# Eighteen scatters of token places put behind the late rows' match matrices, and one expert's input transposes one block later

## The chip, the cores and the metric

The kernel runs on one core of one Trainium2 chip. The metric is device microseconds (us) of one execution, as the median of three runs. TensorE is called PE here, its weight loads PEld, VectorE DVE, ScalarE ACT, GpSimd POOL, and SyncE SP; SP issues most DMAs, POOL issues the indirect ones (a list of rows in, a list of rows out).

## What is computed

Three layers in a row: masked attention (4 batches, 8 heads, 576 positions, head size 64), a mixture of eight experts of which each token takes one, and a two-layer network with a squared ReLU. Cut to what matters:

```python
x = attn_out.transpose(0, 2, 1, 3).reshape(B * S, H * D)     # 2304 tokens x 512
logits = x @ w_gate
e_idx = np.argmax(logits, axis=1)                             # one expert per token
gate_w = softmax(logits)[np.arange(N), e_idx]
eom = 1.0 / (1.0 + np.exp(-(x @ w_output_gate)))
for e in range(E):
    mask = e_idx == e
    h = np.maximum(x[mask] @ w1[e], 0.0)
    out[mask] = gate_w[mask, None] * eom[mask, e, None] * (h @ w2[e])
h = np.maximum(out @ w_in, 0.0)
return h * h @ w_out
```

## The kernel before

**Attention and routing.** Attention runs batch after batch. Its output stays on chip as `xT`; whenever the heads of 128 tokens are done, `gates()` (L555) turns them into rows (`rw`, L568), copies them to `xr`, stores them to the DRAM table `x_d` (L595, SP queue) and reduces the routing logits (`lg`, L572). There are 18 such tiles of 128 tokens in four groups, 0 to 3, 4 to 8, 9 to 12 and 13 to 17. `route()` (L786) takes a group: it finds each token's expert, its place in that expert's bucket (`rk`, `pp`, `posi`, L810 to L825), and queues one **scatter** per tile in the list `scq`: a POOL indirect DMA (L860) that writes 128 token numbers, 4 bytes each, to their places in the DRAM table `tab_d`.

**When a scatter is issued.** `put_place()` (L530) takes one from the list. A scatter of group 0 or 1 stands behind a one-column POOL copy `seen` (L451) that reads a tile of batch 2 or 3, so the first four come in batch 2's attention and the next five in batch 3's. The nine of groups 2 and 3 stand behind `lead["win"]`, the last gather of the first expert's rows.

**The first expert.** Experts run in an order found at run time, largest first, in slots 0 to 7. For slot 0 nothing is read back from `tab_d`: once group 2 is routed, `match_rows()` (L638) computes the first 416 places on PE, and four POOL gathers (`win`, L613) fetch rows from `x_d` into the four `win` buffers. The tokens of group 3 come late: `late_rows()` (L729) compares their places with the places of the slot and makes one **match matrix** `pm` per tile (DVE, L735); PE adds the matched rows up in `lr` (L753, L766), and the split `xh`, `xl` of those sums lets slot 0's first matmul start.

**The next experts.** A slot is eight F1 blocks `f`. In each, `e_l1` makes 12 matmuls to `h` (L1105 to L1107 through a helper), and `e_l2` of two blocks before makes 12 to `y`. At (slot 0, f=1) SP reads slot 1's token list from `tab_d` (`rows_of`, L609), which waits for every scatter; then POOL gathers slot 1's rows (L613), in three tiles of up to 128, and behind them clears `y2T` (L1292, POOL), which the end of slot 0 writes first (L1228). At f=5 of slot 0 `win_split(1)` (L1176) turns the gathered rows over on PE (`wt`, L1183) and splits them into `xh`, `xl` (ACT L1185, DVE L1186) for slot 1's first block. For the later slots this is at f=4.

**What sets the order.** The framework orders each engine's queue by data dependences, program order and its own estimate of times; `tc.issue_after(x)` keeps an instruction behind `x` on its engine. A queue, once ordered, runs strictly in that order: whoever waits holds all behind it. SP's queue carries the weight loads (`rw`, L1079), the early loads of the last layer's weights (`e6wi`, L1120) and the token lists.

Of the kernel before, what the change touches and what calls it, by code (L numbers as in the profile page):

```python
# [20 lines left out]
P = 128  # L21
# [111 lines left out]
def moe_kernel(ctx, tc, q, k, v, wg, wog, w1, w2, w_in64, w_out64, consts, out, dbg=None):  # L133
# [174 lines left out]
    cnt_ev = [0]  # L308
    last_ev, ev_ = {}, [None]
    behind = {}  # L310

    def evac(out_ap, in_ap, scale=None):
        cnt_ev[0] += 1
        if EVP[cnt_ev[0] % len(EVP)]:
            if scale is None:
                ev_[0] = ("v", nc.vector.tensor_copy(out_ap, in_ap))
            else:
                nc.vector.tensor_scalar(out_ap, in_ap, scale, None, op0=ALU.mult)
        else:
            ev_[0] = ("s", nc.scalar.activation(out_ap, in_ap, AF.Copy, scale=1.0 if scale is None else scale))  # L320

# [106 lines left out]
    def unit_s(b, t, u):  # L428
# [19 lines left out]
        )  # L448
        if u == 1 and b >= 2:
            seen = wk.tile([P, 1], F32, name=f"seen{b}", tag="seen", bufs=1)  # L450
            behind[b - 2] = nc.gpsimd.tensor_copy(seen, flat(pr)[:, 0, 0:1])  # L451
        return None, pn
# [60 lines left out]
    q2, q3 = [], []  # L513
    done_all = [False]

    def drain(n2, n3):
        while len(q2) > n2:
            q3.append(unit2(*q2.pop(0)))
        while len(q3) > n3:
            a = q3.pop(0)  # L520
            unit3(*a)
            last_ev[ev_[0][0]] = ev_[0][1]
            done.add((a[0], a[2], a[3]))
            gates()
            if done_all[0]:
                while scq:
                    put_place()


    def put_place():  # L530
        fn, g = scq.pop(0)
        with tc.issue_after((behind[g] if g < 2 else lead["win"]).ins):
            fn()

# [194 lines left out]
    def late_rows(t0, t1, rows):  # L729
# [3 lines left out]
        for t in range(t0, t1):  # L733
# [3 lines left out]
            )  # L737
            pms.append((t, pm))
        with tc.issue_after(lead["pm"].ins):
            while lows:  # L740
# [45 lines left out]
    def route(b, ts, lg, rows):  # L786
# [84 lines left out]
        for i, t in enumerate(ts):  # L871
            scq.append((lambda i=i, t=t: scatter(i, t), b))

# [11 lines left out]
    for b in range(B):  # L885
        t = tiles[b]
        tn = transposes(b + 1, tiles[b + 1]) if b + 1 < B else iter(())
        for n, ku in enumerate(ORDER[b].split()):
# [22 lines left out]
            if b == B - 1 and n >= LN and early and "do" in lead:  # L911
                lead.pop("do")()
                early_load()
                lead["ok"] = 1
            for _ in range(2):
                if scq and (scq[0][1] in behind if scq[0][1] < 2 else "ok" in lead):
                    put_place()
            for _ in range(TN[b][n]):
# [4 lines left out]
        if b + 2 < B:  # L923
            tiles[b + 2] = load(b + 2)
    done_all[0] = True
    while scq:
        put_place()
    drain(0, 0)


# [347 lines left out]
    for k in range(E):  # L1278
        for f in range(NF1):
# [18 lines left out]
            if (k, f) in CONV:  # L1298
# [4 lines left out]
                for j in range(n * len(halves) // len(CONV), (n + 1) * len(halves) // len(CONV)):  # L1303
                    conv_early(j)
            if f == (5 if k == 0 else 4) and k + 1 < E:
                win_split(k + 1)
# [290 lines left out]
```

## Time and profile before

| what | before |
|---|---|
| median of three runs | 801.55 us (800.99 to 802.63) |
| the profiled execution's own time | 803.88 us |
| its span, first to last instruction | 802.1 us |
| PE busy, share of the span | 95% |
| DVE, ACT, POOL busy | 68%, 57%, 24% |
| attention and routing | until about 168 us |
| eight expert slots, then the last layer | from about 168 us |

The profile is one execution. The page gives the busy time of each engine and the chain of work that ended last; the views of the trace give the instructions in order of time, what ended the idle time before each, and busy time by stretch. Times in them are us from the span's start.

### The profile page before, as it was taken

Reading aid. Unit: us, or ns where it says so; the run is one execution under the profiler, and the core shown is the slowest. Engines: PE = TensorE matmul, PEld = TensorE weight load, DVE = VectorE, ACT = ScalarE, POOL = GpSimd, SP = SyncE. Lnnn points to the kernel's source line nnn. Section 1 sums busy time; section 2 is a strip of 40 time slices with the busy share of each in tenths; the row PEclk is TensorE's granted clock in tenths of the full one; section 3 lists DMA queues with packets and bytes.
Section 4 is the critical chain, followed back from the end, with each engine's and each line's share of the span. In section 5 each row is a group of like instructions: output and inputs, shape, how many; then the busy total and the mean of one; then the engine's idle time right before and its main releaser. Section 6 shows DMA issues by size and latency. Waiting matters only on the chain.

```text
span 802.1 us, 14559 instructions
## 1 busy us (share of the span) xinstructions
PE 764.3 (95%) x5409; PEld 684.7 (85%) x5409; DVE 544.4 (68%) x1062; ACT 459.1 (57%) x930; POOL 192.9 (24%) x184
## 2 busy tenths in 40 slices
PE   8899988799999999999999999999999999999995
PEld 4677676589999999999988989888898898899894
DVE  4757677574458578779789777787565579456533
ACT  2645545334546465656767767776565578466543
POOL 6100202436074764431042222003000003000002
PEclk9999999899999999999999999999999999999998
DMA  9999911859488899876554643434223223423002
GB/s 181 172 194 193 148 41 42 169 135 341 155 195 280 187 312 307 288 251 209 166 190 156 193 170 125 163 106 152 93 76 122 73 92 127 149 73 105 14 2 81
DMA packets 113603, 124.87 MB, mean 156 GB/s; under 512 B 42676, under 2 KB 86360, under 8 KB 113528
## 3 DMA queue, kind: packets, MB, share of 16 engines
q1 hardware_dynamic: 103928, 100.50, 45.6%
q0 software_dynamic: 8096, 22.63, 8.4%
q10 hardware_dynamic: 1504, 0.76, 0.5%
q8 instruction: 44, 0.72, 0.4%
q14 instruction: 31, 0.25, 0.1%
HBM read 101.74 MB, written 22.12 MB: 154 GB/s over the span
## 4 chain that ended last, share of the span: by engine, by line
PE 70%; issue 16%; DVE 5%; ACT 4%; DMA 3%; POOL 1%; SPq 1%; another core or an unknown queue 0%; POOLq 0%; ACTq 0%; DVEq 0%
PE o L1107 5%; PE o L1105 5%; PE o L1106 5%; PE h L1105 4%; PE y L1105 4%; PE y L1106 4%; PE y L1107 4%; PE h L1107 4%; PE h L1106 4%; PE rw L568 2%; DMA s0wo<-in_moe_w_out_dram 1%; PE wt L1183 1%; POOL out_dram L1351 1%; PE lr L753 1%; DMA kl<-in_k_dram 1%
## 5 line engine op out<-in xcount | busy, mean ns | idle before, releaser
L1105 PE MATMUL o<-hwo,gh 128*128 128x512 f32 x288 | 113.5, 394 | 1.9 <-ACT gh L1322 1.9
L1106 PE MATMUL o<-lwo,gh 128*128 128x512 f32 x288 | 113.5, 394 | 0.0
L1089 DVE TENSOR_TENSOR lw<-rw,hw 128x1024 fp32r<-128x1024 f32 x62 | 78.2, 1262 | 43.9 <-ACT hw L1085 38.2
L1085 ACT ACTIVATE hw<-rw 128x1024 fp32r<-128x1024 f32 x62 | 66.0, 1064 | 62.1 <-PE h L1106 37.8
L1319 ACT ACTIVATE rl<-rl 128x384 f32<-128x384 f32 x96 | 49.2, 517 | 88.6 <-DVE rl L1317 87.0
L1107 PE MATMUL o<-hwo,gl 128*128 128x512 f32 x288 | 85.0, 395 | 2.2 <-DVE gl L1324 2.2
L1351 POOL DMA_INDIRECT out_dram<-ob,idx x18 | 21.1, 1175 | 271.4 <-ACT ob L1350 266.7
L1105 PE MATMUL h<-xh,hw 128*128 128x416 f32 (+7 forms) x256 | 80.7, 315 | 3.0 <-DVE hl L1205 3.0
L1324 DVE TENSOR_TENSOR gl<-rl,gh 128x384 fp32r<-128x384 f32 x96 | 55.9, 585 | 39.6 <-ACT rl L1323 38.7
L1107 PE MATMUL h<-xh,lw 128*128 128x416 f32 (+7 forms) x256 | 79.4, 310 | 0.0
L1106 PE MATMUL h<-xl,hw 128*128 128x416 f32 (+7 forms) x256 | 79.4, 310 | 0.0
L1106 PE MATMUL y<-hl,hw 128*128 128x416 f32 (+7 forms) x256 | 77.1, 310 | 0.0
L1107 PE MATMUL y<-hh,lw 128*128 128x416 f32 (+7 forms) x256 | 76.6, 310 | 0.0
L1105 PE MATMUL y<-hh,hw 128*128 128x416 f32 (+7 forms) x256 | 67.7, 311 | 0.5 <-ACT hh L1204 0.5
L1105 PEld LDWEIGHTS o<-hwo,gh 128*128 128x128 f32 x288 | 54.2, 188 | 12.3 <-ACT gh L1322 2.9
L1107 PEld LDWEIGHTS o<-hwo,gl 128*128 128x128 f32 x288 | 53.4, 188 | 11.3 <-DVE gl L1324 3.0
L1106 PEld LDWEIGHTS o<-lwo,gh 128*128 128x128 f32 x288 | 54.1, 188 | 9.5
L1105 PEld LDWEIGHTS h<-xh,hw 128*128 128x128 f32 x256 | 48.1, 188 | 4.0 <-DVE hl L1205 3.7
L1323 ACT ACTIVATE rl<-rl 128x384 f32<-128x384 f32 x96 | 50.2, 522 | 2.2
L1322 ACT ACTIVATE gh<-rl 128x384 fp32r<-128x384 f32 x96 | 50.0, 521 | 1.7
L1106 PEld LDWEIGHTS h<-xl,hw 128*128 128x128 f32 x256 | 48.2, 188 | 0.1
L1106 PEld LDWEIGHTS y<-hl,hw 128*128 128x128 f32 x256 | 48.1, 188 | 0.1
(614 smaller groups left out, 1907.7 us busy)
## 6 DMA issues: line engine op xcount, KB each, us to landing
rw<-in_moe_w_dram SPq DMA_DIRECT2D x62, 512.0 KB
rwa<-ws_d SPq DMA_DIRECT2D x24, 512.0 KB
rwb<-ws_d SPq DMA_DIRECT2D x24, 384.0 KB
e6wi<-in_moe_w_in_dram SPq DMA_DIRECT2D x32, 256.0 KB
rwo<-wout_d SPq DMA_DIRECT2D x16, 512.0 KB
x_d<-xr SPq DMA_DIRECT2D x18, 256.0 KB
ws_d<-eo POOLq DMA_DIRECT2D x16, 256.0 KB
s0wo<-in_moe_w_out_dram SPq DMA_DIRECT2D x8, 512.0 KB
```

The lines of the kernel that those rows point to most:

```text
L568: lead["rw"] = nc.tensor.matmul(ps[:, kk, :], xT[:, kd, col : col + P], igw[:, kd, :], start=True, stop=True)
L753: acc["o"] = nc.tensor.matmul(sums[h][:, a, :], parts[t][x][:, 2 * h + a, :], pm, start=(t == t0 and a == x == 0), stop=False,)
L1085: nc.scalar.activation(hi, raw, AF.Copy)
L1089: eng.tensor_tensor(lo, raw, hi.bitcast(F32), op=ALU.subtract)
L1105: kept(nc.tensor.matmul(ps, ah, bh, start=first, stop=False))
L1106: kept(nc.tensor.matmul(ps, ah, bl_, start=False, stop=False))
L1107: kept(nc.tensor.matmul(ps, al, bh, start=False, stop=last))
L1319: nc.scalar.activation(rl[:, :HC], src, AF.Relu)
L1322: nc.scalar.activation(hh[:, :HC], rl[:, :HC], AF.Square)
L1323: nc.scalar.activation(rl[:, :HC], rl[:, :HC], AF.Square)
L1324: nc.vector.tensor_tensor(hl[:, :HC], rl[:, :HC], hh[:, :HC].bitcast(F32), op=ALU.subtract)
L1351: ins = nc.gpsimd.indirect_dma_start(out=out[:, :], out_offset=bass.IndirectOffsetOnAxis(ap=idx[:, gt_, 0:1], axis=0), in_=ob, in_offset=None,
```

## The change

The lists and bookkeeping by which a scatter found its place in attention go: the two `seen` copies in batches 2 and 3, `behind`, `last_ev`, `put_place()` and its calls. After the loop over the batches one `seen` copy on POOL reads the last match matrix, and all 18 scatters stand behind it, one after another. Slot 1's `win_split` moves from f=5 to f=6 of slot 0.

```diff
--- before.py
+++ after.py
@@ -306,18 +306,16 @@
         return t
 
     cnt_ev = [0]
-    last_ev, ev_ = {}, [None]
-    behind = {}
 
     def evac(out_ap, in_ap, scale=None):
         cnt_ev[0] += 1
         if EVP[cnt_ev[0] % len(EVP)]:
             if scale is None:
-                ev_[0] = ("v", nc.vector.tensor_copy(out_ap, in_ap))
+                nc.vector.tensor_copy(out_ap, in_ap)
             else:
                 nc.vector.tensor_scalar(out_ap, in_ap, scale, None, op0=ALU.mult)
         else:
-            ev_[0] = ("s", nc.scalar.activation(out_ap, in_ap, AF.Copy, scale=1.0 if scale is None else scale))
+            nc.scalar.activation(out_ap, in_ap, AF.Copy, scale=1.0 if scale is None else scale)
 
     def transposes(b, t):
         t.update(trs[b % 2])
@@ -446,9 +444,6 @@
         eng.tensor_tensor(
             flat(pn)[:, :, :SM], flat(pr), rc[:, :, None].to_broadcast([P, n, SM]), op=ALU.mult
         )
-        if u == 1 and b >= 2:
-            seen = wk.tile([P, 1], F32, name=f"seen{b}", tag="seen", bufs=1)
-            behind[b - 2] = nc.gpsimd.tensor_copy(seen, flat(pr)[:, 0, 0:1])
         return None, pn
 
     np2 = [0]
@@ -511,7 +506,6 @@
     tiles = {0: load_s(0)}
     load_l(0, tiles[0])
     q2, q3 = [], []
-    done_all = [False]
 
     def drain(n2, n3):
         while len(q2) > n2:
@@ -519,18 +513,8 @@
         while len(q3) > n3:
             a = q3.pop(0)
             unit3(*a)
-            last_ev[ev_[0][0]] = ev_[0][1]
             done.add((a[0], a[2], a[3]))
             gates()
-            if done_all[0]:
-                while scq:
-                    put_place()
-
-
-    def put_place():
-        fn, g = scq.pop(0)
-        with tc.issue_after((behind[g] if g < 2 else lead["win"]).ins):
-            fn()
 
     carry = [None]
     late_ = []
@@ -736,6 +720,7 @@
                 pm, cst[:, C_IO : C_IO + NL], rel[:, t - t0 : t - t0 + 1], None, op0=ALU.is_equal
             )
             pms.append((t, pm))
+            lead["pmt"] = pm
         with tc.issue_after(lead["pm"].ins):
             while lows:
                 lows.pop(0)()
@@ -869,7 +854,7 @@
             scat.append(ins)
 
         for i, t in enumerate(ts):
-            scq.append((lambda i=i, t=t: scatter(i, t), b))
+            scq.append(lambda i=i, t=t: scatter(i, t))
 
     tg = transposes(0, tiles[0])
     for _ in range(2 * 3 + 1):
@@ -911,10 +896,6 @@
             if b == B - 1 and n >= LN and early and "do" in lead:
                 lead.pop("do")()
                 early_load()
-                lead["ok"] = 1
-            for _ in range(2):
-                if scq and (scq[0][1] in behind if scq[0][1] < 2 else "ok" in lead):
-                    put_place()
             for _ in range(TN[b][n]):
                 next(tn, None)
         for _ in tn:
@@ -922,10 +903,13 @@
         tg = iter(())
         if b + 2 < B:
             tiles[b + 2] = load(b + 2)
-    done_all[0] = True
-    while scq:
-        put_place()
     drain(0, 0)
+    seen = wk.tile([P, 1], F32, name="seen", tag="seen", bufs=1)
+    with tc.issue_after(lead["win"].ins):
+        lead["seen"] = nc.gpsimd.tensor_copy(seen, lead["pmt"][:, 0:1].bitcast(F32))
+    with tc.issue_after(lead["seen"].ins):
+        while scq:
+            scq.pop(0)()
 
 
     cp = pss.tile([P, E], F32, name="cntp", tag="sc")
@@ -1302,7 +1286,7 @@
                     conv_load(1)
                 for j in range(n * len(halves) // len(CONV), (n + 1) * len(halves) // len(CONV)):
                     conv_early(j)
-            if f == (5 if k == 0 else 4) and k + 1 < E:
+            if f == (6 if k == 0 else 4) and k + 1 < E:
                 win_split(k + 1)
             if (k, f) in ((E - 2, 5), (E - 1, 0)):
                 split2(0, k + 2 - E)
```

## Rows read from the trace of the kernel before

**Rows 1.** The page: busy by engine, and the chain that ended last by engine

```profile
PE 764.3 (95%) x5409; PEld 684.7 (85%) x5409; DVE 544.4 (68%) x1062; ACT 459.1 (57%) x930; POOL 192.9 (24%) x184
...
PE 70%; issue 16%; DVE 5%; ACT 4%; DMA 3%; POOL 1%; SPq 1%; another core or an unknown queue 0%; POOLq 0%; ACTq 0%; DVEq 0%
```

**Rows 2.** Busy us by stretch: PE, PEld, DVE, ACT, POOL; granted PE clock, DMA share, GB/s

```profile
98.00:124.00 26.00, 23.93 (x369) 18.66 (x367) 19.49 (x72) 13.09 (x49) 1.33 (x2) 1.00 0.15 43
128.00:133.00 5.00, 3.01 (x41) 2.12 (x39) 1.35 (x7) 1.80 (x10) 2.85 (x3) 1.00 0.20 53
...
155.00:163.00 8.00, 7.18 (x37) 5.87 (x36) 6.04 (x16) 3.98 (x7) 4.47 (x4) 0.57 1.22 82
...
174.00:200.00 26.00, 25.94 (x141) 25.31 (x142) 14.85 (x18) 12.59 (x18) 16.16 (x7) 1.00 0.95 307
```

**Rows 3.** Chain of waits, 118 to 176 us: start, length (us), what

```profile
128.85 3.62 another core or an unknown queue
...
150.44 4.19 issue
...
155.06 1.83 PE wt L723 x4
```

**Rows 4.** Timeline of POOL: start, length (us), operation, idle time before and its end

```profile
93.47 0.96 POOL L860 DMA_INDIRECT tab_d<-tok,posi  x1 [0.30 <-issue]
...
125.37 1.01 POOL L860 DMA_INDIRECT tab_d<-tok,posi  x1 [0.16 <-issue]
...
130.50 0.96 POOL L860 DMA_INDIRECT tab_d<-tok,posi  x1 [0.30 <-issue]
145.13 1.00 POOL L613 DMA_INDIRECT win<-x_d,ix  x1 [13.67 <-DVE ix L668]
...
150.14 1.01 POOL L860 DMA_INDIRECT tab_d<-tok,posi  x1 [0.31 <-issue]
...
157.62 0.97 POOL L860 DMA_INDIRECT tab_d<-tok,posi  x1 [2.65 <-DVE rel L731]
...
164.41 0.96 POOL L860 DMA_INDIRECT tab_d<-tok,posi  x1 [0.30 <-issue]
176.70 1.12 POOL L613 DMA_INDIRECT win<-x_d,ix  x1 [11.33 <-PE h L1107]
...
180.67 9.06 POOL L1292 MEMSET y2T<- 128x10688 f32 x1
```

**Rows 5.** Timeline of PE in attention, same columns

```profile
95.34 0.60 PE L501 MATMUL o2s<-ptp,vsp 128*64 128x72 f32 x12 [0.51 <-issue]
...
131.03 0.34 PE L501 MATMUL o3s<-ptp,vsp 128*64 128x72 f32 x3 [1.12 <-issue]
```

**Rows 6.** Timeline of DVE: match matrices, then the work beside the scatters

```profile
157.65 1.48 DVE L735 TENSOR_SCALAR pm<-cst,rel 128x208 fp32r<-128x208 f32 x5
...
162.05 2.35 DVE L1089 TENSOR_TENSOR lw<-r,hw 128x1024 fp32r<-128x1024 f32 x2
```

**Rows 7.** SP's queue: what it waited for, 150 to 200 us; then its timeline

```profile
SPq L609 <- DMA tab_d<-tok,posi: 0.6, 1, 0.6
...
155.28 1.95 SPq L1079 DMA_DIRECT2D rw<-in_moe_w_dram  x3
173.32 1.55 SPq L609 DMA_DIRECT2D ix<-tab_d  x2
```

**Rows 8.** Timeline of PE around slot 0, same columns as Rows 4

```profile
148.66 0.61 PE L723 MATMUL wt<-cst,win 128*128 128x128 f32 x4
...
188.38 0.35 PE L1105 MATMUL h<-xh,hw 128*128 128x416 f32 x1
...
192.31 1.04 PE L1183 MATMUL wt<-cst,win 128*128 128x128 f32 x8
193.10 0.44 PE L1105 MATMUL h<-xh,hw 128*128 128x416 f32 x1
```

**Rows 9.** Timeline of ACT: the first write of y2T

```profile
210.56 1.33 ACT L1228 ACTIVATE y2T<-y 128x416 f32<-128x416 f32 x3
```

## Prediction

> **What bounds the kernel now.** I began with the page. PE is busy for 95% of the span, and the chain that ended last runs through PE for 70% of it and through "issue" for 16% [rows 1]. An edit that adds no PE work can therefore gain only where PE stands idle on that chain, and lose only by making it stand. Next I read busy time by stretch. In an ordinary piece of attention, 98 to 124 us, PE is busy for 23.93 of 26 us and DVE for 19.49; from 174 us on, in the first expert's blocks, PE is busy for 25.94 of 26 us, while the DMA engines are 95% busy at 307 GB/s [rows 2]. So attention has some slack on PE, and slot 0 has none: a PE wait there is paid in full, and its weights and rows come through a DMA system that is nearly full.
>
> Between the two stand the places that the change touches. From 128 to 133 us PE is busy for 3.01 of 5 us and DVE for 1.35, although the DMA engines are only 20% busy [rows 2]. The chain of waits has 3.62 us there that it can put down to no engine, from 128.85 us [rows 3]. On POOL five scatters run from 125.37 to 131.5 us [rows 4]. PE itself has a hole of 1.12 us before 131.03 us in which it waits for no one, and holes of the same kind, the first of 0.51 us before 95.34 us, stand behind the first four scatters, the last of which starts at 93.47 us [rows 4, 5]. That is the reading on which a gain rests: where scatters run in attention, all engines slow down a few us after they start. The trace doesn't say why.
>
> **The change part by part.** The sum is made against the profiled execution's own 803.88 us (span 802.1 us and 1.78 us around it). That is 2.33 us above the median of 801.55, which I take off at the end.
>
> *The scatters leave attention.* Nine scatters and two one-column copies go from POOL's queue there. POOL is not what attention waits for, so their own length gains nothing. What may go is the slowing. For the first four I take one hole of 0.51 us and another like it, 1.0 us in all (bounds 0 and 1.0). For the next five, PE lost little: at its share of 98 to 124 us, 92%, five us hold 4.60 us of work, and 3.01 were done, so 1.7 us of time. DVE, at 75%, would have done 3.75 us and did 1.35, so 3.2 us of time [rows 2]. The chain gives 3.62 [rows 3]. I take DVE's 3.2 us, since the chain runs through DVE on both sides of that hole; bounds 1.7 and 3.6. What is late next is DVE itself, which then works without a pause.
>
> *The first four scatters behind the gathers leave too.* They start from 150.14 us, right behind the slot's gathers [rows 4]. In the chain, 1.83 us lie between the rank matmuls and the DVE step that reads them, with only transposes and filler matmuls in it [rows 3]. It may be the scatters' doing or that of the gathers, which stay: bounds 0 and 1.8, I take half, 0.9 us. The 4.19 us before it [rows 3] begin at 150.44 us, and only one scatter had started by then, 0.3 us before; I count no gain on them.
>
> Gains: 1.0 + 3.2 + 0.9 = 5.1 us, between 1.7 and 6.4.
>
> *All eighteen now run in one train.* They stand behind a POOL copy that reads the last match matrix. DVE ends the five matrices at 157.65 + 1.48 = 159.1 us [rows 6]; with the copy the first scatter starts at about 159.4 us. Behind the waiting copy POOL's queue holds the 18 scatters, slot 1's gathers, the clearing of `y2T` and all later gathers; nothing of attention is left on POOL. Two scatters start (130.50 - 125.37) / 4 = 1.28 us apart where POOL is undisturbed, and (164.41 - 157.62) / 4 = 1.70 us apart beside DVE's splits [rows 4, 6]. DVE's dense work lasts until 164.4 us [rows 6], so I take four gaps of 1.70 and thirteen of 1.28: the last scatter starts at 182.8 us (bounds 181.2 and 188.3).
>
> *The token list of slot 1 waits for all of them.* SP's read of it was issued at 173.32 us and had waited for the scatters to land, though only 0.6 us of that was left to wait [rows 7]. The last scatter had started at 164.41 us, 8.9 us before [rows 4]. The quickest indirect DMA that the rows show is a gather, from 145.13 to the PE transposes that use it at 148.66 us, 3.5 us [rows 4, 8]. I take the middle, 6.2 us: the read is issued at 189.0 us (184.7 to 197.2), 15.7 us later than before. If SP's queue is ordered so that weight loads stand behind this read, they are late with it. I cost that at nothing, since three weight loads for slot 0 go out from 155.28 us [rows 7], long before the read, and the framework may put the next ones ahead of a read that it counts as not ready; should that cover go, it comes with the rival of the late list below.
>
> *Slot 1's rows.* Its first gather started 3.4 us after the read was issued (176.70 - 173.32) [rows 4, 7]; the second follows 1.3 us later. For landing the bounds are the gather's own 3.5 us and the scatter's 8.9 us. I take 5.0, nearer to the gather's row and above it, since the DMA engines are 95% busy then [rows 2]. The first two tiles, which PE's transposes need together, are there at 189.0 + 3.4 + 1.3 + 5.0 = 198.7 us (192.9 to 210.8).
>
> *The transposes one block later.* They stand at 192.31 us; a block is 193.10 - 188.38 = 4.7 us, so they move to 197.0 us [rows 8]. PE runs in order, so a late gather stops it: 198.7 - 197.0 = 1.7 us (0 to 13.8). The same twelve transposes, three ACT copies and three DVE subtractions are issued. They have one block less before slot 1's first matmul. A DVE subtraction of twice that width takes 2.35 / 2 = 1.18 us [rows 6], so three take about 1.8 us, an estimate; that fits into a block, and I cost it at nothing.
>
> *What else moves.* The clearing of `y2T`, 9.06 us on POOL [rows 4], starts behind slot 1's gathers, at about 196.3 us instead of 180.67, and ends at about 205.4. The first write of `y2T` comes at 210.56 us [rows 9], so 5 us of cover are left; gathers of slot 2 behind it have a whole slot. The other bookkeeping issues no instruction.
>
> The sum: -5.1 + 1.7 = -3.4 us, so 800.5 us for a profiled execution and **798.2 us** for the median.
>
> **A rule of the Trainium skill on each side of the sum.** The scatters are the only work in 125 to 131 us that isn't there from 98 to 124 us, and PE stands beside them [rows 2, 5]. The Trainium skill's page "SBUF — State Buffer" (section "SBUF: two separate sides") holds that of the engines only DVE and GpSimd share a port pair, and that PE and ACT never wait on anyone there. By that rule PE's holes are not the scatters' doing through that memory and may stay; this is the second rival. On the other side, scatters beside DVE's two-input work started 1.70 us apart and alone 1.28 [rows 4]. The same section warns that GpSimd can't write its DMA descriptors while DVE holds the shared pair. It speaks against this change, which moves nine scatters out of attention into the splits of the first expert. By it all gaps could be 1.70 us, the first rival's train.
>
> **The rivals.**
>
> *The list comes late: slower.* One mechanism: the train is slow, and PE waits at slot 1's transposes. For it: after four scatters, from 155 to 163 us, the DMA engines moved 82 GB/s though their booked share stood at 1.22, against 307 GB/s at 0.95 from 174 us on [rows 2]; a train of 18 may hold up DMAs for longer, its own landings among them, and those are just when slot 1's rows are fetched. Against it: weight loads and the last stores to `x_d` share that stretch, and the slow ones may have been these. With gaps of 1.70 and a landing of 8.9 us the read is issued at 197.2, the gathers land at 206.9, and PE waits 9.9 us: -5.1 + 9.9 = +4.8, **806.4 us**. It decides from the point where the second gather lands later than 197.0 + 5.1 = 202.1 us.
>
> *The holes in attention stay.* They would belong to something else, or to recording the profile. For it: the cause isn't shown, the DMA engines were nearly idle, and a like delay stands beside the gathers [rows 3]. Against it: the holes come only beside indirect DMAs. Gain 0, cost 1.7: **803.3 us**.
>
> *The transposes don't move.* Before, PE's queue has them ahead of the block that stands before them in the program (192.31 against 193.10) [rows 8], so the framework placed them by its own estimate and may do so again. At 192.3 us PE would wait 6.4 us: -5.1 + 6.4 = +1.3, **802.9 us**.
>
> **How the numbers follow.** My forecast has 45%, the late list 26%, the staying holes 17%, the unmoved transposes 12%. The forecast's own range is 795.5 (most of the gain and no wait) to 800.0 us. A measurement of this kernel can tell about 0.2% from no change, 1.6 us. Faster by more than that: 40 points of the forecast and 5 of the others' lower ends, 45%. Within it: 4 of the forecast and 14 of the others, 18%. Slower: 1, 22, 9 and 5 points, 37%. The range that should hold the time eight times in ten goes from 795.5 to 806.5 us and leaves out the far ends of the gain and of the late list.
>
> **What would show it.** Right: no hole in the chain near 129 us and PE busy there as from 98 to 124; match matrices some 5 us earlier; 18 scatters in one row, ending about 24 us behind them; slot 1's transposes about 38 us behind them with a PE wait under 4 us. Wrong: a hole of the old size in attention without scatters; a PE wait of more than 5 us at slot 1's transposes or first block; DVE or ACT idle for weights from 190 us on; transposes that stand at the old distance from the matrices.

## The result and the profile after

The changed kernel takes 814.02 us (median of six, 812.56 to 815.12) against 801.58 us (800.91 to 803.6) for the kernel before: a ratio of **1.0142, interval 1.0115 to 1.0169**, 12.4 us slower. The forecast was 798.2 us, with 806.5 as the upper end. The profiled execution took 814.18 us with a span of 812.3, 10.2 longer than before. Line numbers of the changed kernel are 16 lower from the routing on, 15 at the scatter.

The page after: busy by engine, and the chain that ended last by engine.

```profile
PE 762.8 (94%) x5409; PEld 684.1 (84%) x5409; DVE 546.8 (67%) x1062; ACT 459.8 (57%) x930; POOL 188.4 (23%) x183
...
PE 66%; issue 19%; DVE 4%; DMA 4%; ACT 3%; SPq 2%; POOL 1%; POOLq 0%; ACTq 0%; DVEq 0%; another core or an unknown queue 0%
```

PE does the same work in a longer span, and "issue" grew from 16% to 19% [rows 1]. The stretches tell where (columns as in [rows 2]):

```profile
128.00:133.00 5.00, 3.73 (x74) 2.96 (x73) 4.81 (x30) 3.06 (x9) 0.00 (x0) 1.00 0.03 7
...
157.00:175.00 18.00, 6.83 (x27) 5.93 (x25) 2.10 (x8) 1.13 (x3) 11.65 (x12) 0.76 0.03 1
174.00:200.00 26.00, 16.53 (x80) 16.34 (x81) 9.39 (x10) 9.16 (x11) 12.95 (x5) 0.75 0.96 272
183.00:188.00 5.00, 4.53 (x16) 4.37 (x17) 3.68 (x3) 3.46 (x4) 1.42 (x2) 0.62 1.01 326
```

Attention is what was hoped: from 128 to 133 us DVE is busy for 4.81 of 5 us, where it was 1.35 [rows 2]. But from 157 to 175 us little but POOL moves: of 18 us PE is busy for 6.83, DVE for 2.10 and ACT for 1.13, and the DMA engines move 1 GB/s. In 174 to 200 us PE does 16.53 us of work where it did 25.94, and when it starts again its granted clock is 0.62 over five us, between the two levels.

Timeline of POOL after: start, length, operation, idle time before and its end.

```profile
136.50 1.17 POOL L597 DMA_INDIRECT win<-x_d,ix  x1 [35.82 <-DVE ix L652]
...
148.31 1.02 POOL L845 DMA_INDIRECT tab_d<-tok,posi  x1 [0.16 <-issue]
...
171.27 0.97 POOL L845 DMA_INDIRECT tab_d<-tok,posi  x1 [0.31 <-issue]
186.28 0.99 POOL L597 DMA_INDIRECT win<-x_d,ix  x1 [14.04 <-issue]
```

Slot 0's first matmul before, then the match matrices on DVE after, slot 0's first matmul after, and PE's first work behind the hole:

```profile
167.73 0.46 PE L1105 MATMUL h<-xh,hw 128*128 128x416 f32 x1
```

```profile
144.41 1.28 DVE L719 TENSOR_SCALAR pm<-cst,rel 128x208 fp32r<-128x208 f32 x5
...
152.65 0.46 PE L1089 MATMUL h<-xh,hw 128*128 128x416 f32 x1
...
183.47 0.72 PE L1089 MATMUL y<-hh,hw 128*128 128x416 f32 x1 [17.81 <-ACT hw L1069]
...
203.15 1.03 PE L1167 MATMUL wt<-cst,win 128*128 128x128 f32 x8
```

Work comes 8.6 us earlier at slot 0's gathers (145.13 to 136.50 [rows 4]), 13.2 at the match matrices (157.65 to 144.41 [rows 6]) and 15.1 at the first matmul of slot 0 (167.73 to 152.65). Then PE waits 17.81 us in one piece. Slot 1's transposes stand at 203.15 against 192.31 us [rows 8]: 10.8 later, 4.7 of it the block by which they were moved, so PE's work is 6.1 late. From 15.1 early to 6.1 late, **slot 0 loses 21 us**. Two executions of the same attention can differ: a pair of traces from the first of the chips below, of the kernel before with only the transposes moved and of the changed kernel, gives 7.2, 11.9 and 13.7 us for the first three, and the later transposes 8.0 late (203.28 against 195.29 us), which makes the loss 21.7. About 4.2 us more go near 275 us: PE's work is 6.0 late at slot 2's transposes (262.06 against 256.04 us) and 10.3 at slot 3's (348.89 against 338.63). There stands the next row of indirect DMAs, two gathers and eight writes of the table `idx_d`, from 263 to 277 us, and beside it ACT is idle for 8.54 us:

```profile
278.09 1.06 ACT L1069 ACTIVATE hw<-rw 128x1024 fp32r<-128x1024 f32 x1 [8.54 <-remote]
```

Three waits end together. SP in the chain of waits, SP's timeline, and ACT's timeline:

```profile
159.92 0.70 SPq L1004
160.66 0.69 SPq L1004
...
174.10 0.69 SPq L1552
174.89 7.45 DMA rw<-in_moe_w_dram
```

```profile
139.78 3.00 SPq L579 DMA_DIRECT2D x_d<-xr  x3
174.89 1.58 SPq L1063 DMA_DIRECT2D rw<-in_moe_w_dram  x3
179.07 1.57 SPq L593 DMA_DIRECT2D ix<-tab_d  x2
```

```profile
160.43 0.52 ACT L1188 ACTIVATE hh<-h 128x416 fp32r<-128x416 f32 x1 [2.07 <-issue]
174.90 0.93 ACT L1188 ACTIVATE hh<-h 128x416 fp32r<-128x416 f32 x2 [13.96 <-remote]
182.36 1.06 ACT L1069 ACTIVATE hw<-rw 128x1024 fp32r<-128x1024 f32 x1 [6.53 <-DMA rw<-in_moe_w_dram]
```

First, **SP's queue order**: before, three weight loads went out at 155.28 us [rows 7]; now eight register reads stand ahead of them (L1004 seven times, L1552 once: expert order and overflow flag). Second, **SP's pace**: from about 158.5 us on nearly every step of these reads, or the pause behind it, takes 0.70 us, so they last from 156.9 to 174.8 us. A read has three steps, a load from on-chip memory, some register arithmetic and a check; before, they took about 0.27, 0.15 and 0.02 us. Beside the row the check takes as long as the load, up to 0.70 us, so it is SP's stepping that slows and not only the read of memory. Third, **the late pick-up**: PE's matmuls to `h` end at 165.66 us, and ACT, for which the trace shows nothing else to wait for, takes them up at 174.90, 9.2 us later; the third group, which ended at 163.39, was taken up no sooner. The trace puts this wait down to no engine ("remote"), so it can't tell a signal of PE that comes late from an ACT queue that steps late. ACT's queue has seven register reads of its own, from 157.0 to 162.8 us; beside such reads the first two groups are taken up 2.6 to 3.1 us late, in the run without scatters too, but they end 12 us before 174.90. All three waits end within 1 us of the landing of the 18th scatter, 174.1 us by its DMA's records.

### The profile page after: what moved, and what is told of

Read it like the earlier page. It is cut to its first block, busy times and chain, and to the rows that moved or that the text cites. A ratio compares the mean times of both kernels' runs of the same rounds, so it can differ in the third digit from the quotient of the medians.

```text
span 812.3 us, 14554 instructions
## 1 busy us (share of the span) xinstructions
PE 762.8 (94%) x5409; PEld 684.1 (84%) x5409; DVE 546.8 (67%) x1062; ACT 459.8 (57%) x930; POOL 188.4 (23%) x183
## 4 chain that ended last, share of the span: by engine, by line
PE 66%; issue 19%; DVE 4%; DMA 4%; ACT 3%; SPq 2%; POOL 1%; POOLq 0%; ACTq 0%; DVEq 0%; another core or an unknown queue 0%
PE o L1091 5%; PE o L1089 5%; PE o L1090 5%; PE y L1090 4%; PE h L1089 4%; PE y L1089 4%; PE y L1091 4%; PE h L1091 4%; PE h L1090 4%; PE rw L552 2%; PE wt L1167 1%; SPq L1004 1%; DMA rw<-in_moe_w_dram 1%; POOL out_dram L1335 1%; DMA kl<-in_k_dram 1%
## 5 line engine op out<-in xcount | busy, mean ns | idle before, releaser
L1089 PE MATMUL y<-hh,hw 128*128 128x416 f32 (+7 forms) x256 | 66.6, 315 | 18.5 <-ACT hw L1069 17.8
L1089 PEld LDWEIGHTS o<-hwo,gh 128*128 128x128 f32 x288 | 54.1, 188 | 12.3 <-ACT gh L1306 2.9
L1089 PEld LDWEIGHTS y<-hh,hw 128*128 128x128 f32 x256 | 44.2, 190 | 19.6 <-ACT hw L1069 18.2
```

Source lines behind the costliest of these rows:

```text
L1089: kept(nc.tensor.matmul(ps, ah, bh, start=first, stop=False))
```

## The experiments

The runs were made on three chips. The result above shows SP's slow steps and the late pick-up by ACT, and so does the first chip (kernel before: 804 us). On the second (794 us) three traces of an unbroken train show neither; on the third (790 us) only trains that were cut ran. Ratios are against the kernel before on the same chip. The theories bear the names that the expectations give them.

**The moved transposes alone.**

```diff
-            if f == (5 if k == 0 else 4) and k + 1 < E:
+            if f == (6 if k == 0 else 4) and k + 1 < E:
```

> The kernel before with one part of the change alone: the second slot's transposes stand one F1 block later (f == 6), the scatters stay where they were. Both theories, which concern the scatters: within 2 us of before, 800 to 803 us, since TensorE waited 1.8 us for the transposes before the change. If the later place of the transposes carried part of the loss, 805 us or more.

First chip: 1.0012 (0.9984 to 1.0039). The transposes move to 195.29 us and PE doesn't wait for them. This part of the change costs nothing.

**Nine scatters left out, in either kernel.** First in the kernel before (groups 0 and 1, those of attention), then in the changed kernel, which leaves a train of nine.

```diff
-            scq.append((lambda i=i, t=t: scatter(i, t), b))
+            if b >= 2:
+                scq.append((lambda i=i, t=t: scatter(i, t), b))
```

> The kernel before without the nine scatters of groups 0 and 1 (their tokens' places stay zero in the table, so the gathered rows are others than the reference's; all else is computed). Theory A (the holes in attention, also the 4.19 us at 150.44, come from scatters beside attention): the first slot's gathers start by about 137 instead of 145.13, the match matrices end by about 146 instead of 159.1, TensorE has no hole near 129 nor near 150, and as SP's order stays as it is the time is 787 to 794 us. Theory B (the prediction's: only the two holes named in it belong to the scatters, 5 us in all): gathers at about 141, 796 to 798 us.

> The changed kernel with half the train: the nine scatters of groups 0 and 1 are left out (their tokens' places stay zero in the table, so other rows are gathered), SP's order stays that of the changed kernel, with the reads of meta ahead of the three weight loads. Theory 1 (the order, with register steps of 0.7 us on SP whatever runs beside them): the weights still go out near 175 and the time stays at 812 to 815 us. Theory 2 (the train slows SP's steps for as long as it runs): nine scatters fewer at 1.275 us end the train some 11.5 us earlier, the weights go out near 163, PE's 18 us hole shrinks to about 6 to 7 us: 801 to 804 us.

Both on the first chip. The kernel before without its early nine: **0.9904** (0.9859 to 0.9949). Its gathers come at 134.74 us instead of 145.13 [rows 4], as early as in the changed kernel: the holes in attention are the scatters' doing. That trace is not of this chip, though. Against the run above, with the same attention on the first chip (142.68 us), the gathers are 7.9 us earlier and slot 0's first matmul 8.0 (157.29 against 165.25 us); the ratio gives 7.7. So nearly all of it arrives, though PE waits 3.8 us for `pm`. From the gathers to that first matmul it is 22.6 us in the kernel before, in the run above and in this one, and 16.1 in both traces of the changed kernel: these 6.5 us come not from the early nine but from taking the other nine out from behind the gathers. The changed kernel with half the train: 0.9983 (0.9956 to 1.001). The framework ordered SP's queue otherwise here, weights first (from 142.46 us), so the run changes two things. What it does show: with nine scatters ACT takes the third group of matmuls up 0.8 us after its end (161.82 and 162.58 us), but PE still waits 7.4 us, since the list's read holds SP until 165.33 us and the fourth weight load stands behind it.

**The order of SP's queue mended.** In the first run the seven order reads are kept behind the third weight load, in the second the flag's read too.

```diff
+            with tc.issue_after(lead["ld"].ins):   # lead["ld"]: slot 0's third weight load
-            oreg[k] = nc.values_load(meta[0:1, k : k + 1], ...)
+                oreg[k] = nc.values_load(meta[0:1, k : k + 1], ...)
...
+    with tc.issue_after(lead["ld"].ins):           # second run only
+        flag = nc.values_load(meta[0:1, 3 * E : 3 * E + 1], ...)
```

> The changed kernel with one thing put back: on SP's queue the three weight loads rw of slot 0 stand ahead of the eight register reads of meta again, as they did before the change; the train of 18 scatters stays where the change put it. Theory 1 (the order on SP is the loss): the weights go out at about 143 us, behind the stores of x, instead of 174.89, so TensorE's hole of 18.16 us ahead of 183.47 closes and the 13 us that attention gained are kept: 790 to 796 us. Theory 2 (the train itself freezes the other engines and queues until its last scatter at 174.1, whatever stands on SP): ACT still sees TensorE's matmuls of 165.66 only at about 174.9, and PE stays idle for some 9 us of the 18: 804 to 808 us.

> The changed kernel with all eight register reads of meta on SP behind the three weight loads (in the first such kernel one read, that of the overflow flag, was still ahead of them and held them until 161.31). Theory 1 (order alone): the weights go out at about 143 and land by 150, no hole is left: 790 to 796 us. Theory 2 (the train): the weights land early, but TensorE's completions and the list's read still wait for the last scatter near 174, so 8 to 11 us of hole stay: 804 to 809 us.

First run, first chip: 1.0055 (1.0026 to 1.0084). One read was still ahead, and the weights went out at 161.31 us; yet ACT stands as before:

```profile
161.31 3.61 SPq L1064 DMA_DIRECT2D rw<-in_moe_w_dram  x3
```

```profile
174.16 0.93 ACT L1191 ACTIVATE hh<-h 128x416 fp32r<-128x416 f32 x2 [12.50 <-remote]
```

So the order is one holder and not the only one. Second run, second chip: 1.0144 (1.0087 to 1.0202), although the weights left early and ACT took no matmuls up late there:

```profile
141.02 2.73 SPq L1064 DMA_DIRECT2D rw<-in_moe_w_dram  x3
176.78 1.55 SPq L593 DMA_DIRECT2D ix<-tab_d  x2
178.59 1.67 SPq L1064 DMA_DIRECT2D rw<-in_moe_w_dram  x3
```

Now the read of slot 1's list stands on SP for 21.2 us, until the last scatter has landed, and the next weights behind it; PE waits 14.6 us at `h`. This is the cover "the framework may put the next ones ahead" taken away, on a chip without the other effects.

**Places 64 bytes apart.** `tab_d` holds one 4-byte place per 64 bytes; positions are multiplied by 16 and lists read with that stride. It asks whether writes to neighbouring words are what slows. Of the changed kernel, of it with the mended order, and of the kernel before on the second and on the first chip:

```diff
-    tab_d = dram.tile([E * NT, 1], I32, name="tab_d")
+    tab_d = dram.tile([E * NT * 16, 1], I32, name="tab_d")
...
-                out_offset=bass.IndirectOffsetOnAxis(ap=posi[:, t : t + 1], axis=0),
+                out_offset=bass.IndirectOffsetOnAxis(ap=posw[:, t : t + 1], axis=0),  # 16 * posi
```

> The changed kernel with the places of the table 64 bytes apart instead of 4 (the list has 16 words a place, the scatters still write one word of 4 bytes each, 18 of them, in the same train, in the same order on every queue; the positions are multiplied by 16 once on VectorE; the table that is cleared at the start is 16 times as large, 1.18 MB). Theory W (neighbouring words of one expert's bucket, written by different DMA engines, get in each other's way in memory and hold up every other transfer, register read and completion): the 0.7 us steps on SP between 158 and 174.8 fall to about 0.2, the three weights go out by about 161, the completions of TensorE arrive on time, and the hole of 18.16 us shrinks to some 3 to 6: 799 to 804 us. Theory N (the number of small writes or of their descriptors does it, wherever they land): nothing changes, 812 to 816 us.

> Both of the last two edits on the changed kernel: reads of meta behind the three weight loads, and places 64 bytes apart. Theory W: the whole gain of the attention stage (13 us) is kept, less what the later weights lose behind the list's read, which still waits for 18 scatters at 1.275 us: 790 to 798 us. Theory N: as the kernel with the order alone.

> The kernel before with its places 64 bytes apart (one small multiply on VectorE per group of tiles, the cleared table 16 times as large), scatters where they were, inside attention. Theory W: the holes of TensorE near 95, 129 and 150 close without any scatter being moved, as in the kernel that left nine scatters out: 792 to 798 us. Theory N: the holes stay, 801 to 805 us.

> Again the kernel before with places 64 bytes apart and scatters inside attention, now beside the kernels that keep the change: if the holes in attention come from neighbouring words alone, moving the scatters has nothing left to win, and this one is as fast as the kernel with all three or faster, since its list is complete 20 us earlier: 791 to 795 us against 801.6 of the kernel before.

Second chip: the changed kernel 1.0145 (1.0088 to 1.0202), with the mended order 1.0179 (1.0109 to 1.0249), the kernel before **0.9904** (0.9875 to 0.9934). In the first of these SP's steps are short (0.15 to 0.3 us). PE waits 8.5 us for `hl` and 3.9 us for `hw`, while ACT stands 9.50 us for the fourth weight load, which left SP at 174.99 us, behind the list's read. I first took this for the effect of the spacing. The same edit on the first chip showed that it is the chip. The kernel before with spread places, 128 to 133 us, first chip, then second:

```profile
128.00:133.00 5.00, 2.91 (x45) 2.19 (x42) 1.02 (x5) 2.42 (x11) 3.18 (x4) 1.00 0.21 55
```

```profile
128.00:133.00 5.00, 4.12 (x77) 3.48 (x76) 4.28 (x25) 1.66 (x3) 0.00 (x0) 1.00 0.08 13
```

On the first chip DVE does 1.02 us of work, as in [rows 2], and the gathers come at 145.76 us; on the second the stretch is whole and they come at 134.51. On the first chip the ratio is 0.995 (0.9924 to 0.9976). There, spread places don't cure the holes. They gain 0.5 to 1%, on both chips where they were tried, and **of the versions that leave nothing out, this is the one that is faster than both kernels**; by what path it gains was not settled.

**The list read from POOL's queue.** On top of the mended order, POOL itself reads the lists of slots 1 and 2, so nothing of SP waits for the train. Then the same with spread places, and with spread places but SP's order as the change has it.

```diff
-        nc.sync.dma_start(ix[:, :nw], tab_e[...])
+        eng.dma_start(ix[:, :nw], tab_e[...])      # nc.gpsimd for slots 1 and 2
```

> The changed kernel with two edits on its queues, places still 4 bytes apart: the eight register reads of meta behind the three weight loads, and the reads of the places lists of slots 1 and 2 issued by POOL behind its own scatters instead of by SP (which until now stood at the list from 155.5 to 176.8 with the fourth weight behind it). Theory 3 (what is left of the loss is the fourth weight of slot 0 behind the list's read on SP): the fourth and fifth weights go out as soon as their buffers are free, about 165 us, and the hole of 14 to 16 us ahead of the first y matmuls falls to 3 us or less: 794 to 799 us against 801.6 of the kernel before. Theory 2 (the train's freeze of completions and transfers is enough by itself): PE still idles 8 us or more until the train ends near 174, 801 us or more.

> The changed kernel with all three: reads of meta behind the three weight loads, lists of slots 1 and 2 read by POOL, places 64 bytes apart. Theory 3 with W: nothing of the hole of 18.16 us is left and the 13 us of attention are kept: 787 to 793 us against 801.6 of the kernel before. If some fourth cause holds TensorE, a hole stays ahead of 180 us and the time is above 797 us.

> The changed kernel with places 64 bytes apart and the lists of slots 1 and 2 read by POOL, but SP's order left as the change made it (eight reads of meta ahead of the three weight loads). This prices the order alone: the weights go out at about 161 instead of 143 and land near 164.7, so PE waits about 4 us for them and later ones are some 3 us late: 792 to 797 us against 801.6 of the kernel before, 3 to 5 us above the kernel with all three. If the order costs nothing once the register steps are quick, within 1 us of the kernel with all three.

First chip: 1.0066 (1.0038 to 1.0093), 1.0016 (0.9993 to 1.0039), 1.0067 (1.0041 to 1.0092). In the second run the weights left from 142.66 us and no list stood on SP, but:

```profile
174.09 0.52 ACT L1197 ACTIVATE hh<-h 128x416 fp32r<-128x416 f32 x1 [15.17 <-remote]
```

```profile
PE y L1098 <- ACT hw L1078: 14.4, 1, 14.4
```

With two holders gone, the third alone keeps PE for 14.4 us. In the third run SP's reads ran at 0.7 us again and PE waited 17.0 us; the very same queue order had been through with them at 161.05 us on the second chip with the same train. In the first run of the three most of the wait fell at the transposes (12.3 us for slot 1's rows): the late list of the prediction. That run is also an exception: though nothing cut its 18 scatters, PE is busy for 19.10 of the 25 us from 150 to 175 us, and ACT takes the matmuls up 2.7 us late and no later. Its row has a pause of its own, 2.58 us instead of 1.28 between the ninth start (159.98 us) and the tenth (162.56). What made the pause the trace doesn't show.

**The train cut, turned round, left out.** Four runs on the first chip. One cuts the train: nine scatters, the clearing of `y2T` (9 us on POOL), nine more behind slot 0's third block. It is built on the version with the mended order, POOL's lists and spread places, and it also reads slot 1's list at a later block (f=3). One turns every scatter into an indirect read of the same 128 places (the table stays empty). One leaves all scatters out. These two are built on the mended order with POOL's lists. The last is the changed kernel itself.

```diff
-        while scq:
+        for _ in range(9):
             scq.pop(0)()
...
+            if (k, f) == (0, 2):
+                with tc.issue_after(lead["seen2"].ins):    # a POOL copy of this block's hl
+                    while scq:
+                        scq.pop(0)()
```

```diff
-                out=tab_d[:, :], out_offset=bass.IndirectOffsetOnAxis(ap=posi[...], axis=0),
-                in_=tok1[:, t : t + 1], in_offset=None,
+                out=zero[:, t : t + 1], out_offset=None,
+                in_=tab_d[:, :], in_offset=bass.IndirectOffsetOnAxis(ap=posi[...], axis=0),
```

> The kernel with all three edits (reads of meta behind the weights, lists read by POOL, places 64 bytes apart), and the train cut in two: nine scatters behind the late rows' match matrices as now, the clearing of y2T (9 us on POOL) behind them, and nine more behind the third F1 block of slot 0. If the freeze comes from an unbroken train of more than about eight scatters: SP's steps stay below 0.3 us, ACT's relu of slot 0 is never later than 3 us behind its matmuls, the hole of 14.4 us ahead of the first y matmuls is gone; instead the list of slot 1 is complete only near 187 and PE waits up to 12 us at the second slot's transposes: 798 to 804 us against 801.6 of the kernel before. If every scatter freezes for as long as it flies, however they are spaced: both trains show 0.7 us steps and 805 us or more.

> The kernel with reads of meta behind the weights and lists read by POOL, places 4 bytes apart, in which each of the 18 scatters is turned into an indirect read: the same 128 places of 4 bytes, from the same table, into a scratch column (so the table stays zero and other rows are gathered). If the writes to memory make the freeze: no 0.7 us steps, no late completions, no hole ahead of the first y matmuls: 790 to 798 us against 801.6 of the kernel before. If the building of the indirect descriptors (128 per instruction, POOL busy 0.97 us of every 1.275) makes it: the freeze stays as it is, 806 to 812 us.

> The kernel with reads of meta behind the weights and lists read by POOL, with no scatter at all (the table stays zero, other rows are gathered): the floor of this arrangement. If the train is the whole of the loss: TensorE has no hole between the match matrices and slot 1, 784 to 790 us against 801.6 of the kernel before. If something else in the new order holds TensorE, a hole stays there: above 795 us.

> The changed kernel itself, unaltered, beside these three: 812 to 816 us against 801.6 of the kernel before on a chip that shows the freeze; on a chip without it (register steps of 0.3 us or less) the hole is the order and the list read alone and the ratio is the same within 0.5%.

Ratios in this order: **0.9982** (0.9954 to 1.0011), 1.0014 (0.9982 to 1.0046), **0.9847** (0.9789 to 0.9905), 1.0119 (1.0052 to 1.0186). Stretches of the cut train, of no scatters, and of the changed kernel:

```profile
150.00:175.00 25.00, 24.74 (x140) 23.84 (x139) 18.45 (x51) 11.12 (x16) 21.79 (x14) 1.00 0.79 241
```

```profile
150.00:175.00 25.00, 23.48 (x134) 22.55 (x134) 18.52 (x51) 10.58 (x15) 7.02 (x6) 1.00 0.78 247
```

```profile
150.00:175.00 25.00, 11.33 (x62) 10.15 (x61) 7.20 (x41) 3.05 (x7) 16.29 (x17) 0.85 0.09 1
```

With the train cut in two, PE is busy for 24.74 of 25 us, and ACT takes matmuls up at most 3.2 us after their end; uncut, PE has 11.33. The second nine start only between 171.88 and 182.96 us, so the stretch holds 11 or 12 of the 18; but from 172 to 186 us, beside the second nine, PE is busy for all of the 14 us. The hole belongs to the unbroken train. It isn't writing to memory, for with reads it stays, at its old place, with nothing that waits for these reads to land (PE still waits 8.6 us):

```profile
175.54 0.93 ACT L1187 ACTIVATE hh<-h 128x416 fp32r<-128x416 f32 x2 [13.86 <-remote]
```

What the cut train still loses is at the transposes:

```profile
PE wt L1177 <- DMA win<-x_d,ix: 6.7, 2, 6.1
```

**The version with two trains, improved.** Two variants on the third chip: group 0's four scatters back in attention, so that five and nine are left behind the match matrices; and half the clearing (4.5 us) as the pause between trains of nine.

```diff
+                if "seen0" in lead and len(scq) and NTILE - nput[0] > 14:   # four in batch 2
...
-                    nc.gpsimd.memset(y2T, 0.0)
+                    nc.gpsimd.memset(y2T[:, : KD // 2], 0.0)   # other variant; rest behind the list
```

> The kernel with two trains, with the four scatters of group 0 put back inside attention (where the kernel before has them), so that the first train behind the match matrices is five long, the second nine, the clearing of y2T between them. The list is complete some 5 us earlier than with nine and nine, which takes away most of the 6.7 us that PE waited for the second slot's rows; the four cost attention about 2 to 3 us again. If the two trains stay free of the freeze: 795 to 799 us against 801.6 of the kernel before, faster than both. If four scatters in attention freeze what runs beside them by more than 5 us, 801 us or more.

> The kernel with two trains of nine, with only half of the clearing of y2T (4.5 us) between them and the other half behind the list's reads. If a pause of 4.5 us is enough: no relu of slot 0 later than 3 us behind its matmuls, the list some 4.5 us earlier, PE's wait at the second slot's transposes 2 to 3 us instead of 6.7: 796 to 800 us against 801.6 of the kernel before. If the freeze needs the longer pause to clear, the hole ahead of the first y matmuls is back: 804 us or more.

1.0129 (1.0078 to 1.018) and 1.0073 (1.0047 to 1.0099). Both lose. The kernel before is 14 us faster on this chip than on the first; that it lacks the holes from which a gain could come would explain it, but its trace was not taken there. In the second PE still waits 4.2 us at the transposes. In the first a new stall appears, POOL's clearing over routing's small DVE operations (the first is the CAST; those behind it wait their turn on DVE):

```profile
152.18 9.02 POOL L1302 MEMSET y2T<- 128x10688 f32 x1
```

```profile
153.21 8.03 DVE L955 CAST meta<-mf 128x8 int32<-128x8 f32 x1
153.28 7.95 DVE L970 TENSOR_TENSOR over<-mf,cst 128x8 f32<-128x8 f32 x1
...
161.29 0.17 DVE L971 TENSOR_SCALAR over<-over 128x8 f32<-128x8 f32 x1
```

The CAST of eight elements takes 8 us and ends about with the clearing (152.18 + 9.02 = 161.20), and three more operations in order behind it do too; PE waits 9.3 us for `hl` behind them.

## Why the prediction was wrong, point by point

**The gain: right in its cause, mis-sized.** The holes went with the scatters, so the rival that they stay is false. The term "5.1 us, between 1.7 and 6.4" measured about 15 at slot 0's first matmul (13.7 in the other pair of traces). The two holes of attention, taken at 1.0 + 3.2, came to 8.6 us at the gathers: PE's visible holes were only the part of the slowing in which PE had nothing queued. The last term, 0.9 us with a bound of 1.8, came to 6.5 (15.1 - 8.6; 6.5 in the other pair too), and there the step that failed is "I count no gain on them": of the 4.19 us of [rows 3] PE's wait at that place (`rk`) is 1.42 us after. One scatter had started before that hole, and I asked whether it could have caused it; I did not ask what the four behind it were doing while it lasted.

**The train: right.** It was to start at about 0.3 us behind the matrices; the copy is 2.39 us long here, so it starts 2.6 behind them (148.31 against 145.69). Scatters are (171.27 - 148.31) / 17 = 1.35 us apart, 1.28 for most, and not 1.70 beside the splits. The changed kernel's DVE had little to do then, 2.10 of 18 us, but the cut train is 1.28 us apart too for the most part, beside a DVE that is busy for 18.45 of 25 us. Single scatters do last longer, 1.8 to 2.2 us, each one that starts inside a running two-input subtraction on DVE: those at 149.64 us after and at 150.61, 160.76 and 178.29 in the cut train end about 0.85 us behind that subtraction. So the rule in the prediction that GpSimd's descriptors wait for DVE fits single scatters, but it did not set the row's pace.

**The weights: the failed step.** "I cost that at nothing, since three weight loads for slot 0 go out from 155.28 us [...], long before the read [...]". That nothing was the step that failed. The loads that were to be the cover were not ahead any more: behind the edit the framework put the eight register reads before them, and they left at 174.89 us; PE's wait of 17.81 us ends with them and with ACT's late pick-up, where the sum had 1.7 us of wait in all, and that at slot 1's transposes. The sentence in front of it had the right question, an SP queue ordered otherwise, and asked it only of the list's read. The order is not the whole of it: with seven of the eight reads put behind the weights PE still waits 11.2 us on the first chip. The order mended in full shows the next layer on the second chip: with the weights at 141.02 us the list's read does hold the later ones, and PE waits 14.6 us.

**What the sum did not contain.** A price for work that merely runs beside the train. SP's reads take 0.7 us a step, and ACT takes matmuls up 9.2 us late. The rows had the sign of it: "all engines slow down a few us after they start", said of four and five scatters. I took the slowing as fixed to attention, as something that the change removes; it belonged to the scatters and moved with them, and on the first chip 18 in a row cost more than the same in shorter rows. The rival of the late list spoke of DMAs that the train holds up, and put the wait at slot 1's rows; the wait came a block into slot 0.

**Why mending one thing gave little.** The loads behind SP's slow reads, the loads behind the list's read, and ACT's late pick-up all come free about when the train's last scatter lands. Removing one or two left the rest to hold PE until then (ACT's waits of 12.50 and 15.17 us, 21.2 us of list read). On the first chip every trace in which 14 or more indirect DMAs follow each other at 1.28 us shows ACT's long wait; those whose row is halved, cut, absent, or paused by itself don't. The version without scatters, 0.9847, is some 12 us faster than the kernel before, but it has the mended order, POOL's lists and the moved transposes in it as well, so 12 us is about what all scatters may cost there, not a measured price.

**The other rivals.** The transposes did move, by 10.8 us, the 4.7 of a block included, and at no cost in the kernel before. The late list exists, at 12.3, 6.7 and 4.2 us where the hole was reduced or gone; in the changed kernel it is hidden by the hole, for slot 1's rows are there before PE comes to 203.15 us.

**The clock.** It was in no term. While PE waits, the granted clock falls, and the first matmuls after 183.47 us follow each other at 0.35 us instead of 0.19, the lower level. At 0.62 over five us this is some 1.9 us of the 21; the hole itself is 17.8, and a wait for `hl` behind it 1.8.

**Open.** What the train and these engines share was not found: the spacing of the places and writing are excluded, and that the row is unbroken is shown to matter. How long it must be is not shown. SP's steps become slow about 10 us after a row's first scatter, about at the eighth (148.31 and 158.5 us after), so a row of nine ends as they begin; and at 263 to 277 us ten indirect DMAs are enough: ACT is idle for 8.2 to 8.6 us beside them in the result's trace and in all ten of the first chip that have the same spacing there. Why the second chip shows neither slow steps nor a late pick-up is open too. The difference shows again at that row of ten: with the same spacing ACT is idle for 3.5 us in five traces of the second and third chip. On the second chip the change loses 1.4% with spread places or mended order, by SP's queue alone; the unedited changed kernel was not run on it.

## What to carry to other kernels

A cover counts only in the queue order that the edit will produce: of each instruction that is to hide something, ask what the framework may now put ahead of it on its queue. If a kind of work slows everything around it, moving it moves the slowing: price what runs beside its new place, and as one unbroken row it may cost more than in pieces. When several waits end at the same instant, mending one shows nothing; look for what ended there, and cut that.

## What the runs showed of the hardware

**A long unbroken row of indirect DMAs delays the engines beside it, on one chip and not on another.** With 18 in a row, 1.28 us apart, ACT waits 12.5 to 15.2 us for matmuls that have ended long before, and SP's steps take 0.70 us each, even a check that takes 0.02 us otherwise. With nine in a row, with the 18 cut in two, and with one pause of 2.58 us in the middle, ACT takes matmuls up within 3.2 us. The long wait comes with places 4 or 64 bytes apart and with reads as with writes. On the second chip, with 18 in a row, ACT takes the third and fourth group up within 0.1 us of their end. The Trainium skill's page "DMA: Bandwidth & Descriptors" (section "Anatomy of one DMA — SWDGE (gpsimd) path") says that one can emit a lot of descriptors before an added cost shows. For POOL that agrees, nearly all its scatters keep to 1.28 us, up to the last; for the engines beside it the cost is large (11.33 us of PE work in 25 us, against 24.74 with the row cut).

**A POOL memset held a DVE CAST of eight elements to its end**, 8 us, and three operations in order behind it, in one run on the third chip. In the cut train the clearing ran beside two-input subtractions on DVE that took their usual 1.2 us. The Trainium skill's page "SBUF — State Buffer" (section "SBUF: two separate sides") calls the port pair that DVE and GpSimd share an exclusive lock, held for the whole instruction; the 161.20 us at which both end agree with it. The same section says that PE and ACT never wait on anyone there; ACT's 13.96 us without a reason in the trace is then not that memory, but no run here shows what it is.
